# The last shifted copy of each VectorE quad made in place by an accumulating DMA from Pool

## The chip, the cores and the metric

The kernel runs on one core of one Trainium2 chip. The metric is the device time of one execution in microseconds; the median of three runs of the kernel before is 867.45 us (867.33 to 867.89). A change of the time is a change of that median.

## The reference

One transformer block with adaptive layer norm, 2048 tokens of 512 features, 32 heads of 16, a feed-forward layer of 1792, all in bf16:

```python
mod = (silu(c) @ w_mod).reshape(1, 6, 1, 512)        # sa, ca, ga, sb, cb, gb
h = layernorm(x) * (1 + ca) + sa
q, k, v = split(h @ wqkv)                            # 32 heads, 16 each
o = softmax(q @ k.T * 16 ** -0.5) @ v
x = x + ga * (o @ wo)
h = layernorm(x) * (1 + cb) + sb
x = x + gb * ((gelu(h @ w_gate) * (h @ w_up)) @ w_down)
```

The heavy part is the softmax: 32 x 2048 x 2048 exponentials (134 million), on 128 lanes.

## The kernel before

**Units, rounds, banks.** The query tokens are cut into six sets (SETS: three of 512, one of 256, two of 128). A *unit* is a set (or the two last ones together) and a group of four heads (`qd`, 0 to 7), so the four heads' keys share the 128 rows of TensorE. A *round* of a unit is one stretch of key tokens: its four scores (one for each head) fill four PSUM banks of 128 x 512. There are 2048 such banks in all, and `stream` emits them in chunks of up to three (CH = 3) into the two halves of the six-bank tile ps_sc. While ACT takes the exponential of one half into the ring E, TensorE writes the scores of the other.

**PV products.** After the exp, `pv_mms` multiplies the four banks of a round with the values (`vaug`, each head's 16 columns and a column of ones for the denominator) and accumulates the unit in ps_pv. When all rounds of a unit are done, `unit_end` copies ps_pv to osb, sends the denominators through two DRAM scratch tensors (SP's queue: scr_den, den, scr_rec, rb), and VectorE multiplies (onorm).

**Quads.** Part of the exponentials is made without ACT. For a round of keys at or beyond key tile T0 = 12, the four banks can be taken by VectorE: one `tensor_scalar` per bank (L338 is the helper that records it; L313 records matmuls, L326 activations) turns the score into the bits of a bf16 number, which is a piecewise linear approximation of the exponential. Such a round is a *quad*. Its bits lie in one of the NK = 3 buffers `kq` (128 x 2048 uint16: two in the tensor dreg, one in mreg). To smooth the approximation, the same bits are used five times: as they are, and with the four constants SHIFT = (26, 51, 77, 102) added to the bits. Each shifted copy is a `tensor_scalar` add over 128 x 2048 uint16 from `kq` into one of the NS = 4 buffers `sq` (in mreg), and is multiplied with the values scaled to match (`vs`). So a quad has five PV products instead of one; it costs VectorE four evictions of 128 x 512 from PSUM and four copies of 128 x 2048, and takes four banks off ACT. In a chunk that carries a bank of a quad, ACT's exp covers two banks (128 x 1024) in place of three (128 x 1536).

**The order is planned while the kernel is built.** The program is recorded by a planner that keeps a modelled clock for each engine (`free`), with a price for every instruction and DMA (`model`, L246), and emits each engine's instructions in a fixed order with semaphore waits. `stream` (L1117) is the loop: it takes the earliest thing that TensorE can do (scores of the next chunk, a PV product, side work, or a filler matmul that keeps TensorE busy), asking `probe` when the operands would be ready. VectorE's and SP's small steps wait in a list of tasks; `background` (L1032) lets SP and VectorE take those whose operands the model holds ready, by `urgency`. A quad is started or continued in a chunk only if the model has VectorE free soon enough:

```python
if len(mem) == CH and "modB" in self.have and self.free["dve"] < t + 700:
```

`shift_task` (L1391) enters the four shifted copies as VectorE tasks when the fourth bank has been evicted. A `kq` buffer comes free when all five products of the quad are done.

**Side work.** Projections of q, k, v, the output projection, the second layer norm and the feed-forward layer of earlier sets are generators (`plan`) whose matmuls go into the bank ps_mi between the chunks. What is left of the last sets' feed-forward layer runs in `tail` (L1455), after the last scores.

Of the kernel before, what the change touches and what calls it, by code (L numbers as in the profile page):

```python
# [6 lines left out]
ALU = mybir.AluOpType  # L7
# [4 lines left out]
U16 = mybir.dt.uint16  # L12

P = 128
# [20 lines left out]
CH = 3  # L35
# [2 lines left out]
assert NSL % CH == 0  # L38
LEAD = 5
T0 = 12  # L40
NK = 3
CREDIT = 1024
NS = 4
AHEAD = 24
FLOW = 3
URGENT = 9
# [11 lines left out]
SHIFT = (26, 51, 77, 102)  # L58
# [20 lines left out]
class _Recorder:  # L79
# [166 lines left out]
    def model(self, op, t, cost):  # L246
        eng = op.eng
        if op.stream not in COMPUTE:
            size, run = cost
            self.free[eng] = t + 450  # L250
            self.dma_free = max(t + 900, self.dma_free) + size / (320 if run >= 1024 else 245 if run >= 512 else 200)
            op.t1 = self.dma_free + (1000 if run > 64 else 1500)
        elif eng == "pe":
            cols, rows, tp = cost
            mode = 0 if tp is None else (1 if rows == 32 else 2)
            t = max(t, self.pe_issue)
            if mode != self.pe_mode:
                t = max(t, self.pe_end + 105)
            q = range(16)
            if mode == 1:  # L260
                q = range(tp[0] // 8, tp[0] // 8 + 4)
            elif mode == 2:
                q = range(tp[1] // 32, 16, 4)
            t = max(t, max(self.tile_free[i] for i in q))
            end = t + max(cols, 64) / 2.4
            for i in q:
                self.tile_free[i] = end
            self.pe_mode, self.pe_issue, self.pe_end = mode, t + (4 if mode else 27), max(self.pe_end, end)
            self.free[eng] = t
            self.log.append((t, cols if mode == 0 else cols / 4))  # L270
            op.t1 = end + 158
        else:
            self.free[eng] = t + cost
            op.t1 = t + cost + (107 if eng == "act" else 92)
# [93 lines left out]
    def bn_aggr(self, out, in_):  # L368
        return self.rec("dve", lambda e: e.bn_aggr(out, in_), [in_], [out], cost=90)

    def dma(self, eng, out, in_, sem, noncontig=False):
        def fn(e):
            if noncontig:
                with self.nc.allow_non_contiguous_dma(reason="small strided transfer"):
                    return e.dma_start(out, in_)
            return e.dma_start(out, in_)  # L376
        n = mybir.dt.size(out.dtype)
        for _, k in out.ap:
            n *= int(k)
        run = min(int(a.ap[-1][1]) * mybir.dt.size(a.dtype) for a in (out, in_))  # L380
        return self.rec(eng, fn, [in_], [out], dma=sem, cost=(n, run))

    def emit(self, final):
        for s in self.count:
# [34 lines left out]
class _Kernel(_Recorder):  # L419
# [12 lines left out]
    def alloc(self):  # L432
# [14 lines left out]
        mreg = sb("mreg", [P, 2 * NDC * F], BF16)  # L447
        self.wst = [[mreg[:, 1024 * (2 * x + b):1024 * (2 * x + b) + 1024].rearrange("p (a n) -> p a n", a=NDC)
                     for b in range(2)] for x in range(2)]
        self.sq = [mreg[:, 4096 + 2048 * i:6144 + 2048 * i] for i in range(NS)]  # L450
        self.wmod = mreg[:, 0:NDC * 3072].rearrange("p (a n) -> p a n", a=NDC)
        dreg = sb("dreg", [P, NFC * D], BF16)
        self.tb1 = dreg[:, 0:8 * D].rearrange("p (b t n) -> p b t n", b=2, t=4)
# [6 lines left out]
        self.wu += [dreg[:, 1024 * i:1024 * i + 1024].rearrange("p (a n) -> p a n", a=NDC) for i in range(4, 7)]  # L460
        self.wd = [self.xs[:, 2 * i:2 * i + 2, :] for i in range(6)]
        self.wd.append(hreg[:, NFC * 256 + 1024:NFC * 256 + 2048].rearrange("p (f n) -> p f n", f=2))
        self.kq = [dreg[:, 0:2048], dreg[:, 2048:4096], mreg[:, 12288:14336]]
        self.vs = sb("vs", [P, len(SHIFT), NKT - T0, H * VW], BF16)
        self.wo = sb("wo", [P, 8, D], BF16)
        self.E = sb("E", [P, NSL, 512], BF16)
# [26 lines left out]
        self.mi = ps("ps_mi", [P, 512], FP32)  # L493
        self.scr1 = self.dram("scr_den", [4, 2048], FP32)
        self.scr2 = self.dram("scr_rec", [4, 2048], FP32)


    def prologue(self):
        sp, act, pe, dve, pool = "sp", "act", "pe", "dve", "pool"
# [20 lines left out]
        self.memset(dve, self.pv[:, :], 0.0)  # L520
        self.memset(dve, self.scp[:, SC - 1, :], 0.0)
        self.warm_up(7)
        self.memset(pool, self.ident[:, :], 0.0)
        self.affine_select(self.ident[:, :], [[-1, P]], ALU.not_equal, 1.0, 0, 1)
        self.memset(pool, self.rm4, 1.0)
# [4 lines left out]
        self.memset(pool, self.vaug[:, :, :].rearrange("p t (h c) -> p t h c", c=VW)[:, :, :, DH:VW], 1.0)  # L530
        self.memset(pool, self.rb[:, :], 0.0)

        for dc in range(NDC):
            self.mm(self.scp[:, 0, dc:dc + 1], self.crow[0:1, P * dc:P * dc + P], self.ones[0:1, 0:1])
        self.act(self.tcol[:, :], self.scp[:, 0, 0:NDC], ACT.Tanh, scale=0.5)
# [494 lines left out]
        return n  # L1030

    def background(self, t):  # L1032
        while self.step("sp", max(self.free["sp"], t) + 40):
            pass
        while self.free["dve"] <= t + 150 and self.step("dve", max(self.free["dve"], t) + 40):
            pass

    def force(self):
        if not self.step("sp", None) and not self.step("dve", None):
            assert self.step("act", None)  # L1040

    def plan(self, ends, nsplit):
# [74 lines left out]
    def stream(self):  # L1117
# [26 lines left out]
        for u in units[2:]:  # L1144
            n, kpb = NKT * u[3] // 512, 512 // u[3]
# [12 lines left out]
        group = {u: max(0, i - 1) for i, u in enumerate(units)}  # L1158
        cg = 0
        left = {u: 0 for u in units}  # L1160
        for u, r, g0 in rounds:
# [3 lines left out]
        quads = []  # L1165
        wait = []
        self.quad_free = list(range(NK))
        self.sq_free = list(range(NS))
        cand = [k for k, (u, r, g0) in enumerate(rounds)
                if u not in units[:2] and r * (512 // u[3]) >= T0]  # L1170
        quad = None

        def take(n):
            r, i = [], pos
# [56 lines left out]
        def pv_do(x):  # L1231
            nonlocal rp, cg
            _, kind, k, rnd, i, src, q = x
            u = rnd[0]
            pv(rnd, i, src)
            begun.add(u)
            left[u] -= 1
            if kind == 0:
                assert k == next(open_rounds())
                rp = k + 1  # L1240
                self.plain[u] -= 1
            else:
                q["ready"].remove((i, src))
                q["n"] -= 1
                if i:
                    self.sq_free.append(q["slots"].pop(i))
                if q["n"] == 0:
                    wait.remove(q)
                    self.quad_free.append(q["k"])
            if left[u] == 0:  # L1250
                self.unit_end(u, acc_of(u))
                if all(left[v] == 0 for v in units if group[v] == cg):
                    cg += 1

        early, late = self.weight_parts()
        while cg <= group[units[-1]]:
# [16 lines left out]
            if tq is not None and tq <= t + 30:  # L1273
# [6 lines left out]
                    self.mm(self.scp[:, s0, :], *filler)  # L1280
                    continue
                g = None
                if len(mem) == CH and "modB" in self.have and self.free["dve"] < t + 700:
                    while quad is None and cand and rounds[cand[0]][2] < pos + AHEAD:
                        cand.pop(0)
                    overdue = {x[1][1] for x in self.tasks if x[1] is not None and x[1][0] == "shift" and self.plain[x[1][1]] <= LATE}
                    if quad is not None:
                        if not overdue - {quad["rnd"][0]}:
                            g = quad["rnd"][2] + quad["j"]
                    elif (not overdue and cand and self.quad_free and (pos < ends[2] or self.credit < CREDIT) and rounds[cand[0]][2] < pos + 96 and self.backlog() < BACK  # L1290
                          and ("vs", rounds[cand[0]][0][1] // 2) in self.have
                          and all(k in self.have for k in self.keys(seq[rounds[cand[0]][2]]))):
                        rnd = rounds[cand.pop(0)]
                        quad = {"rnd": rnd, "j": 0, "k": self.quad_free.pop(0), "ready": [], "n": NS + 1, "slots": {}}
                        left[rnd[0]] += NS
                        self.plain[rnd[0]] -= 1
                        g = rnd[2]
                        vec.update(range(g, g + 4))
                        mem, after = take(CH)
# [14 lines left out]
                if g is not None:  # L1314
                    j = quad["j"]
                    kq = self.kq[quad["k"]]
                    self.ts("dve", kq[:, 512 * j:512 * j + 512].bitcast(U16), self.scp[:, s0 + n, :], 128 / OCT, SHIFT_C,
                            ALU.mult, ALU.add)
                    quad["j"] = j + 1
                    if j == 3:  # L1320
                        quad["ready"].append((0, [kq[:, 512 * x:512 * x + 512] for x in range(4)]))
                        wait.append(quad)
                        for i in range(NS):
                            self.shift_task(quad, i)
                        quad = None
                if self.work and pos >= self.work[0][1]:
# [11 lines left out]
            if w is not None and pos >= w[1]:  # L1338
                ts = self.probe(w[4][1])
                n = w[4][0]  # L1340
# [50 lines left out]
    def shift_task(self, q, i):  # L1391

        def f():
            s = self.sq_free[0]
            self.ts("dve", self.sq[s].bitcast(U16), self.kq[q["k"]].bitcast(U16), float(SHIFT[i]), None, ALU.add)
            if self.probing is None:
                self.sq_free.pop(0)
                q["slots"][i + 1] = s
                q["ready"].append((i + 1, [self.sq[s][:, 512 * x:512 * x + 512] for x in range(4)]))
        self.task([f], ("shift", q["rnd"][0]), lambda: bool(self.sq_free))  # L1400

    def osb_span(self, u):

# [197 lines left out]
```

## Time and profile before

| | before |
|---|---|
| median of 3 runs | 867.45 us (867.33 to 867.89) |
| profiled execution, span | 868.7 us |
| ACT busy | 834.9 us, 96% |
| PE busy | 801.4 us, 92% |
| DVE (VectorE) busy | 694.5 us, 80% |
| POOL busy | 4.5 us |
| mean granted TensorE clock | 0.996 |
| ACT exps from ps_sc, three banks / two banks | 380 / 312 |
| DVE evictions of a quad's bank / shifted copies | 284 / 284 |

The profiled execution has no time of its own beside its span; the span is 1.25 us above the median of the runs. PE is the matmul side of TensorE, PEld its weight loads, ACT ScalarE, DVE VectorE, POOL GpSimd, SP the engine that issues nearly all DMAs. An instruction's duration includes a part in which it overlaps its predecessor on the same engine, so durations of one engine can add up to more than its busy time. In a list of groups each row has the line, the engine, the operation, the tiles (out <- in), the count, then busy us and mean ns of one, and the idle time before it with what ended it. In a list of waits each row has who waited for whom, us in total, how often, and the longest. 71 quads follow from the 284 evictions.

### The profile page before, as it was taken

The numbers are of one execution on the slowest core, as the hardware profiler recorded it, in microseconds if no ns is written. First come the engines' busy times: TensorE is split into PE (matmuls) and PEld (weight loads), VectorE is DVE, ScalarE is ACT, GpSimd is POOL, SyncE is SP. The second block draws the span as 40 slices with busy tenths as digits, with TensorE's granted clock in tenths as the row PEclk, the third lists the DMA queues.
The fourth block names the chain that finished last, engine by engine and source line by source line (L and its number), as shares of the span: only waits on it lengthen the run. The fifth ranks groups of instructions, "written<-read, shape, count | busy, mean of one in ns | idle before, by whom it ended". The sixth has DMA issues, their size and how long they took to land.

```text
span 868.7 us, 27825 instructions
## 1 busy us (share of the span) xinstructions
PE 801.4 (92%) x12558; PEld 283.4 (33%) x12563; DVE 694.5 (80%) x1315; ACT 834.9 (96%) x746; POOL 4.5 (1%) x12
## 2 busy tenths in 40 slices
PE   7889999999998999999999999999998899988977
PEld 3333332322222222222222222222343233345555
DVE  6855788888889899989899999988987674586574
ACT  4999999999999999999999999999999999999992
POOL 1000000000000000000000000000000000000000
PEclk9999999999999999999999999999999999999999
DMA  8101000000001212110001212120234231500000
GB/s 272 45 17 24 6 9 9 10 9 8 3 15 42 78 33 57 45 45 21 15 15 50 70 33 57 34 57 8 59 91 118 68 85 37 151 13 8 21 6 13
DMA packets 63665, 38.08 MB, mean 44 GB/s; under 512 B 17374, under 2 KB 61403, under 8 KB 63547
## 3 DMA queue, kind: packets, MB, share of 16 engines
q1 hardware_dynamic: 63544, 36.31, 14.6%
q8 instruction: 98, 1.61, 0.8%
q14 instruction: 21, 0.16, 0.1%
q10 hardware_dynamic: 2, 0.00, 0.0%
HBM read 33.68 MB, written 2.61 MB: 42 GB/s over the span
## 4 chain that ended last, share of the span: by engine, by line
ACT 78%; PE 14%; DVE 4%; DMA 2%; SPq 1%; issue 1%; DVEq 0%
ACT E L326 76%; PE ps_sc L313 6%; PE ps_mi L313 5%; PE ps_pv L313 3%; ACT wreg L326 3%; DVE mreg L338 1%; DMA mreg<-in_w_mod_dram 1%; SPq L376 1%; DMA rb<-scr_rec 1%; DMA scr_rec<-rden 0%; DVE dreg L338 0%; DVE kme L338 0%; DVE wreg L330 0%; DVE kmo L338 0%; DVE st L366 0%
## 5 line engine op out<-in xcount | busy, mean ns | idle before, releaser
L326 ACT ACTIVATE E<-ps_sc 128x1536 bf16<-128x1536 f32 (+2 forms) x698 | 808.3, 1355 | 13.8 <-PE ps_sc L313 13.6
L313 PE MATMUL ps_sc<-qT,kmo 32*128 32x512 bf16 (+2 forms) x1408 | 179.5, 323 | 12.4 <-ACT E L326 11.1
L313 PE MATMUL ps_sc<-qT,kme 32*128 32x512 bf16 (+2 forms) x1344 | 177.6, 332 | 13.4 <-ACT E L326 10.5
L313 PE MATMUL ps_pv<-E,vaug 128*17 128x512 bf16 (+2 forms) x2360 | 173.5, 322 | 4.2 <-ACT E L326 2.3
L338 DVE TENSOR_SCALAR dreg<-ps_sc 128x512 uint16<-128x512 f32 x192 | 132.5, 690 | 35.3 <-PE ps_sc L313 33.0
L338 DVE TENSOR_SCALAR mreg<-dreg 128x2048 uint16<-128x2048 uint16 x192 | 125.7, 681 | 1.6 <-PE ps_pv L313 1.6
L313 PE MATMUL ps_mi<-wreg,mreg 128*32 128x512 bf16 (+2 forms) x1600 | 109.2, 361 | 9.7 <-DVE wreg L343 4.0
L313 PE MATMUL ps_pv<-mreg,vs 128*17 128x512 bf16 (+2 forms) x1312 | 99.4, 351 | 1.8 <-DVE mreg L338 1.2
L313 PEld LDWEIGHTS ps_sc<-qT,kme 32*128 32x128 bf16 x1344 | 46.3, 91 | 133.7 <-ACT E L326 103.5
L313 PEld LDWEIGHTS ps_sc<-qT,kmo 32*128 32x128 bf16 x1408 | 48.4, 91 | 126.6 <-ACT E L326 100.6
L313 PEld LDWEIGHTS ps_pv<-E,vaug 128*17 128x17 bf16 x2360 | 53.4, 89 | 94.1 <-issue 64.2
L338 DVE TENSOR_SCALAR mreg<-ps_sc 128x512 uint16<-128x512 f32 x92 | 63.4, 690 | 17.9 <-PE ps_sc L313 16.8
L338 DVE TENSOR_SCALAR mreg<-mreg 128x2048 uint16<-128x2048 uint16 x92 | 61.2, 684 | 0.2 <-PE ps_pv L313 0.2
L313 PEld LDWEIGHTS ps_mi<-wreg,mreg 128*32 128x32 bf16 x1600 | 33.4, 95 | 60.4 <-issue 20.4
L347 DVE CAST wreg<-ps_mi 128x512 bf16<-128x512 f32 x51 | 35.0, 687 | 17.9 <-PE ps_mi L313 17.8
L343 DVE SCALAR_TENSOR_TENSOR wreg<-wreg,ps_mi 128x512 bf16<-128x512 bf16 x51 | 34.8, 683 | 11.1 <-PE ps_mi L313 7.6
L313 PEld LDWEIGHTS ps_pv<-mreg,vs 128*17 128x17 bf16 x1312 | 29.9, 89 | 30.8 <-DVE mreg L338 14.2
L313 PE MATMUL ps_mi<-hreg,wreg 128*32 128x512 bf16 x480 | 38.5, 383 | 0.7 <-DVE vaug L347 0.3
L313 PE MATMUL ps_mi<-wo,onorm 128*32 128x512 bf16 x480 | 37.4, 383 | 0.2
L330 DVE TENSOR_TENSOR wreg<-wreg 128x1024 bf16<-128x1024 bf16 (+1 forms) x60 | 35.7, 603 | 0.7
L313 PE MATMUL ps_sc<-xs,ident 128*32 128x512 bf16 (+1 forms) x281 | 25.0, 385 | 9.2 <-ACT E L326 8.9
L330 DVE TENSOR_TENSOR onorm<-osb,rb 128x512 bf16<-128x512 f32 (+2 forms) x43 | 23.6, 549 | 11.9 <-DMA rb<-scr_rec 11.6
(144 smaller groups left out, 591.3 us busy)
## 6 DMA issues: line engine op xcount, KB each, us to landing
mreg<-in_B_w_up_dram SPq DMA_DIRECT2D x25, 256.0 KB, 3.3
mreg<-in_B_w_gate_dram SPq DMA_DIRECT2D x21, 256.0 KB, 2.9
rb<-scr_rec SPq DMA_DIRECT2D x96, 32.0 KB, 1.8
mreg<-in_B_w_down_dram SPq DMA_DIRECT2D x12, 256.0 KB, 2.7
dreg<-in_B_w_down_dram SPq DMA_DIRECT2D x9, 256.0 KB, 4.0
mreg<-in_w_mod_dram SPq DMA_DIRECT2D x1, 2048.0 KB, 12.3
out_dram<-xs SPq DMA_DIRECT2D x16, 128.0 KB, 1.7
xs<-in_A_x_dram SPq DMA_DIRECT2D x3, 512.0 KB, 6.4
```

Source lines behind the costliest of these rows:

```text
L313: return self.rec("pe", lambda e: e.matmul(out, lhsT, rhs, start=start, stop=stop, tile_position=tp), [lhsT, rhs], [out], cost=(n, int(rhs ...
L326: return self.rec("act", lambda e: e.activation(out, in_, func, scale=scale, **kw), rd, wr, cost=self.cost("act", out, [in_], "act"))
L330: return self.rec(eng, lambda e: e.tensor_tensor(out, a, b, op), [a, b], [out], cost=self.cost(eng, out, [a, b], "tt"))
L338: return self.rec(eng, lambda e: e.tensor_scalar(out, a, s1, s2, **kw), rd, [out], cost=self.cost(eng, out, [a], "ts") + (60 if len(rd) > ...
L343: return self.rec("dve", lambda e: e.scalar_tensor_tensor(out, a, s, b, op0=op0, op1=op1), rd, [out], cost=self.cost("dve", out, [a, b], " ...
L347: return self.rec(eng, lambda e: e.tensor_copy(out, in_), [in_], [out], cost=self.cost(eng, out, [in_], "ts"))
L376: return e.dma_start(out, in_)
```

## The change

The kernel after has a fourth `kq` buffer (in the place of the fourth `sq` buffer, so there are NQ = 3 of those). Only three of a quad's four shifted copies are made as before. The fourth, the largest shift, is made in place: once the quad's plain PV product has been put on TensorE's queue, `last_task` enters a task that adds 102 to the bits in `kq` itself. While the unit still has at least FAR = 5 plain rounds to do, the task is a DMA issued by Pool with `accum_op=add`, whose source is a row of 2048 uint16 in DRAM, broadcast to the 128 partitions; otherwise it is a VectorE add in place. A copy that is made after the in-place add takes the difference of the shifts (`q["at"]`). The row in DRAM is written once, in the prologue, from a small memset in E. The planner's model has a price for such a DMA: it holds Pool for 1.5 us, and its result is there 6.5 us after its issue (DMA_ADD). `background` and `force` serve Pool's tasks as they do SP's. A unit that is not yet in turn must leave one `sq` buffer free. And the condition for VectorE's part in a chunk counts from ACT's time instead of TensorE's.

```diff
-NK = 3
+NK = 4
 CREDIT = 1024
 NS = 4
+NQ = 3
+DMA_ADD = 6500
+FAR = 5
...
             size, run = cost
+            if eng == "pool":
+                self.free[eng] = t + 1500
+                op.t1 = t + DMA_ADD
+                return
...
-    def dma(self, eng, out, in_, sem, noncontig=False):
+    def dma(self, eng, out, in_, sem, noncontig=False, add=False):
         def fn(e):
+            if add:
+                return e.dma_start(out, in_, accum_op=ALU.add)
...
-        return self.rec(eng, fn, [in_], [out], dma=sem, cost=(n, run))
+        return self.rec(eng, fn, [in_, out] if add else [in_], [out], dma=sem, cost=(n, run))
...
-        self.sq = [mreg[:, 4096 + 2048 * i:6144 + 2048 * i] for i in range(NS)]
+        self.sq = [mreg[:, 4096 + 2048 * i:6144 + 2048 * i] for i in range(NQ)]
...
-        self.kq = [dreg[:, 0:2048], dreg[:, 2048:4096], mreg[:, 12288:14336]]
+        self.kq = [dreg[:, 0:2048], dreg[:, 2048:4096], mreg[:, 12288:14336], mreg[:, 10240:12288]]
...
+        self.scrc = self.dram("scr_shift", [1, 2048], U16)
...
+        step = self.E[0:16, 0, 0:P].bitcast(U16)
+        self.memset(dve, step, SHIFT[NS - 1])
...
+        self.dma(pool, self.scrc.rearrange("o (p n) -> (o p) n", p=16), step, "cs")
...
-        while self.step("sp", max(self.free["sp"], t) + 40):
-            pass
+        for x in ("sp", "pool"):
+            while self.step(x, max(self.free[x], t) + 40):
+                pass
...
+        self.begun = lambda u: group[u] <= cg
...
-                if i:
+                if i == 0:
+                    self.last_task(q, self.plain[u] >= FAR)
+                if i in q["slots"]:
                     self.sq_free.append(q["slots"].pop(i))
...
-                if len(mem) == CH and "modB" in self.have and self.free["dve"] < t + 700:
+                if len(mem) == CH and "modB" in self.have and self.free["dve"] < max(t + 400, self.free["act"]) + 900:
...
-                        for i in range(NS):
+                        for i in range(NS - 1):
                             self.shift_task(quad, i)
...
-            self.ts("dve", self.sq[s].bitcast(U16), self.kq[q["k"]].bitcast(U16), float(SHIFT[i]), None, ALU.add)
+            self.ts("dve", self.sq[s].bitcast(U16), self.kq[q["k"]].bitcast(U16), float(SHIFT[i] - q["at"]), None, ALU.add)
...
-        self.task([f], ("shift", q["rnd"][0]), lambda: bool(self.sq_free))
+        self.task([f], ("shift", q["rnd"][0]), lambda: len(self.sq_free) > (not self.begun(q["rnd"][0])))
+
+    def last_task(self, q, far):
+
+        kq = self.kq[q["k"]]
+
+        def f():
+            if far:
+                self.dma("pool", kq.bitcast(U16), self.scrc.broadcast_to([P, 2048]), "ad%d" % q["k"], add=True)
+            else:
+                self.ts("dve", kq.bitcast(U16), kq.bitcast(U16), float(SHIFT[NS - 1]), None, ALU.add)
+            if self.probing is None:
+                q["at"] = SHIFT[NS - 1]
+                q["ready"].append((NS, [kq[:, 512 * x:512 * x + 512] for x in range(4)]))
+        self.task([("pool" if far else "dve", f)], ("add" if far else "shift", q["rnd"][0]))
```

More of the change, by code (lines that the diff above doesn't have):

```diff
@@ L1038, in force @@
     def force(self):
-        if not self.step("sp", None) and not self.step("dve", None):
+        if not self.step("sp", None) and not self.step("pool", None) and not self.step("dve", None):
             assert self.step("act", None)
@@ L1167, in stream @@
         self.quad_free = list(range(NK))
-        self.sq_free = list(range(NS))
+        self.sq_free = list(range(NQ))
         cand = [k for k, (u, r, g0) in enumerate(rounds)
@@ L1293, in stream @@
                         rnd = rounds[cand.pop(0)]
-                        quad = {"rnd": rnd, "j": 0, "k": self.quad_free.pop(0), "ready": [], "n": NS + 1, "slots": {}}
+                        quad = {"rnd": rnd, "j": 0, "k": self.quad_free.pop(0), "ready": [], "n": NS + 1, "slots": {}, "at": 0}
                         left[rnd[0]] += NS
```

## The prediction

> **What bounds the kernel now.** I read the page first: busy shares, then the chain that ended last.
>
> ```profile
> span 868.7 us, 27825 instructions
> PE 801.4 (92%) x12558; PEld 283.4 (33%) x12563; DVE 694.5 (80%) x1315; ACT 834.9 (96%) x746; POOL 4.5 (1%) x12
> ACT 78%; PE 14%; DVE 4%; DMA 2%; SPq 1%; issue 1%; DVEq 0%
> ```
>
> ACT is busy 96% of the span and carries 78% of the chain; Pool does nothing after the start. The second view, the groups by shape, gives the prices; the third, the waits, says who waits in the steady part.
>
> ```profile
> L326 ACT ACTIVATE E<-ps_sc 128x1536 bf16<-128x1536 f32 x380 | 543.4, 1557 | 1.5 <-PE ps_sc L313 1.4
> L326 ACT ACTIVATE E<-ps_sc 128x1024 bf16<-128x1024 f32 x312 | 316.8, 1125 | 3.4 <-PE ps_sc L313 3.4
> L338 DVE TENSOR_SCALAR dreg<-ps_sc 128x512 uint16<-128x512 f32 x192 | 132.5, 690 | 35.3 <-PE ps_sc L313 33.0
> L338 DVE TENSOR_SCALAR mreg<-dreg 128x2048 uint16<-128x2048 uint16 x192 | 125.7, 681 | 1.6 <-PE ps_pv L313 1.6
> ```
>
> ```profile
> DVE dreg L338 <- PE ps_sc L313: 33.0, 102, 1.2
> DVE mreg L338 <- PE ps_sc L313: 16.8, 49, 1.5
> ACT E L326 <- PE ps_sc L313: 13.6, 14, 2.1
> DVE onorm L330 <- DMA rb<-scr_rec: 11.6, 7, 4.2
> ```
>
> The exps wait before only a handful of their 692 runs, so ACT sets the pace. Each quad takes four banks off ACT: its four chunks have two banks instead of three. A table of windows (us from the start; PE, PEld, DVE, ACT, POOL busy, clock, DMA share, GB/s) shows where VectorE has room:
>
> ```profile
> 200.00:300.00 100.00, 93.37 (x1123) 26.15 (x1122) 88.60 (x160) 99.95 (x92) 0.00 (x0) 1.00 0.11 29
> 500.00:600.00 100.00, 94.36 (x1155) 25.75 (x1156) 90.89 (x151) 98.85 (x90) 0.00 (x0) 1.00 0.15 41
> 700.00:800.00 100.00, 92.76 (x1946) 40.70 (x1950) 63.98 (x136) 100.00 (x85) 0.00 (x0) 1.00 0.21 58
> ```
>
> Up to 600 us VectorE is about 90% busy, ACT full, PE at 93 to 94%. So three engines are near their limit together, and what is taken from one is soon asked of the next. The chunk pace is about 1.1 us (92 ACT instructions in 100 us).
>
> **The change, part by part.** Counts of the changed kernel come from the order of its built instructions.
>
> *More quads.* 71 quads become 79: 32 chunks go from three banks to two (1536-column exps 380 to 348, 1024-column ones 312 to 344). Each saves ACT 1557 - 1125 = 432 ns, in all 13.8 us. All of it lies on the chain.
>
> *VectorE.* 32 more evictions at 690 ns are +22.1 us; shifted copies fall from 284 to 250 (13 of them in place), 34 x 682 ns = -23.2 us. A wash: -1.1 us, not counted.
>
> *PE.* The additional quads' shifted products come to 24 more groups of four 512-column matmuls and 32 of 128 columns. At 0.21 us for a group that follows another (eight matmuls take 0.60 us in the timeline, four 0.39), the former are 5 us; the latter, at a quarter, 2 us. The 128x512 filler matmuls into ps_mi and ps_sc fall by 112, 28 groups or 6 us. A wash again, but fillers run only where PE is empty, so PE has that much less room to catch up. They also keep the clock up; with PE above 90% busy otherwise I price that at nothing.
>
> *Tail.* After the last score matmul the old order has 64 of the 128-column matmuls ps_mi<-wreg,mreg left; the new order has 128, and 64 of ps_mi<-wreg,qT more. So two more up-projection groups are still due when the exps end: the faster exp stream outruns the side work.
>
> ```profile
> 842.69 1.11 PE ps_mi L313 x64
> 845.00:868.70 23.70, 18.31 (x216) 13.16 (x219) 11.87 (x28) 5.16 (x11) 0.00 (x0) 1.00 0.04 12
> ```
>
> In the chain 64 such matmuls took 1.11 us, so two groups are 2.2 us; their VectorE and tanh steps (a 0.69 cast, a 0.69 product, five tensor products at 0.42, two 0.29 scalars, a tanh of 0.78) add 4.8 if nothing hides them. The window shows an idle ACT there, and no cover but the last sets' own work. Between 2.2 and 7.0 I take the middle, 4.5 us.
>
> *VectorE's turn later in a chunk.* An eviction may now start 0.90 us after ACT is free for the chunk, and ends at 1.59. The scores of that half of ps_sc can follow only then: 0.39 us of PE later is 1.98. A two-bank chunk and the next two-bank chunk take ACT 2 x 0.90 us (the timeline has four 1024-column exps in 3.79 us with the last one's 1.12: (3.79 - 1.12) / 3 = 0.89), so ACT idles 0.2, with the semaphores perhaps 0.3; behind a three-bank chunk nothing. In the old trace 151 of 284 evictions waited for their scores (102 + 49 above), so most are not late. I let the 32 new ones be late, half of them before a two-bank chunk: 16 x 0.3 = 5 us, between 0 and 10 if all 32 pay.
>
> *66 accumulating DMAs.* Each adds one 4 KB row, read 128 times, onto 128 x 2048 uint16 (512 KB). No row shows such a DMA, nor any issued by Pool. The nearest:
>
> ```profile
> mreg<-in_B_w_up_dram SPq DMA_DIRECT2D x25, 256.0 KB, 3.3
> mreg<-in_w_mod_dram SPq DMA_DIRECT2D x1, 2048.0 KB, 12.3
> xs<-in_A_x_dram SPq DMA_DIRECT2D x3, 512.0 KB, 6.4
> dreg<-in_B_w_up_dram SPq DMA_DIRECT2D x3, 256.0 KB, 5.3
> ```
>
> Below, half the bytes land in 3.3 us; above, source, old value and result together are 1.5 MB, under the 2 MB of w_mod with 12.3 us. I take 6.4, the row with the same destination size, which shared its queues at the start. The planner lays the order out for DMA_ADD = 6.5 us: it puts the products that need the sum at the first moment when it believes them there. Between an add and the first PE matmul that waits for it stand 3 or 4 chunks for 4 adds, 5 for 15, 6 for 15, 7 for 17, and 8 to 12 for 15; at 1.1 us, five are 5.5 to 6.6 us with the broken ones at the ends. So an early landing gains nothing, and a late one stalls PE, which is in order: behind the waiting product stand the scores of the next chunks, and ACT runs dry once its one filled half of ps_sc is done (0.90 to 1.33 us). In 25 cases VectorE waits for a landing too, with evictions behind it. The same load lands at 3.3 and at 5.3 us above, a spread of 2. With a mean of 6.4 and half that spread either way, I let 34 adds (those with six chunks or fewer) lose 0.2 us on average after the reserve: 7 us. Ends: 0 if all land in time; 24 if those 34 run 1 us late and lose 0.7 each.
>
> On SP's side 39 chains of small DMAs (scr_den, den, scr_rec, rb) now meet the adds on the same engines. Seven waits of VectorE for rb cost 11.6 us before. If the seven become ten, each 0.5 us longer and the new ones as long as one old wait's third, that is some 3 us; 0 to 10.
>
> Weighed against the skill: Pool's row is 4.5 busy us, all near the start, so no row shows Pool beside VectorE's 2048-column copies. The Trainium skill, SBUF — State Buffer, section "SBUF: two separate sides", says that a DMA from GpSimd waits for its descriptors while VectorE runs a two-port operation. By that rule, landings would come up to a copy or two later, which is the third rival.
>
> *At nothing:* the first DMA that writes the addend (Pool ends its memsets at 5.14 us, the first exp reads and writes at 17.67; 12 us of cover); the fourth buffer (it only lets a quad stay longer); the uint16 memset.
>
> Sum: -13.8 + 4.5 + 5 + 7 + 3 = +5.7 us without the rule. The span of 868.7 is 1.25 us above the median 867.45, so the difference is applied to the median: 873.2, rounded to 873.
>
> **Rivals.** About 0.2% (1.7 us) can be told from no change.
>
> 1. *The adds land inside the plan, with no trouble on SP's queue.* -13.8 + 4.5 + 5 = -4.3: 863.1 us. For it: 256 KB loads at 3.3 us, a DMA share of 0.11 to 0.15 in the main stage. Against it: nothing in the order gives margin. Decided by landings under 6.5 us. The Trainium skill, DMA: Bandwidth & Descriptors, section "Anatomy of one DMA — SWDGE (gpsimd) path", fits 2.0 us plus bytes at 436 GB/s, an estimate of 3.2 us for a plain copy of this size; by it the plan would hold, but no run here shows the accumulating kind. Chance 0.30.
> 2. *Losses and gain cancel within 1.7 us.* 867.5 us. Chance 0.15.
> 3. *Landings at 8 us or more.* A descriptor writer held up by VectorE's copies, or a third pass over the bytes: 6.4 and two copies at 0.68 are 7.8. At 8, 1.5 past the plan, 51 adds with seven chunks or fewer lose 1.5 less half a chunk (0.6), 0.9 each, 46 us in place of the 7: 867.5 + 5.7 + 39 = 912 us. The Trainium skill's rule above would speak for it. Chance 0.15.
>
> **The numbers.** The forecast, slower by 2 to 23 us, has 0.40: own range 869.2 to 890. Faster 0.30, same 0.15, slower 0.55. The range runs from 862 to 893: it leaves out rival 3 and the best end of rival 1.
>
> **What would show it.** Exps 348 and 344; the PE waits for DMA into dreg and mreg a new row of several us, ACT's waits for ps_sc far above 13.6 us; the add's landing near 6.4 us. Wrong if ACT's waits stay below 20 us and no engine waits for the adds (rival 1), or if the landing row says 8 or more (rival 3). The tail is wrong if the time from the last exp of three banks or two to the end does not grow.

## The result and the profile after

The changed kernel takes 945.55 us (median of four runs, 943.22 to 950.23) beside 867.39 us of the kernel before: a ratio of 1.0905, interval 1.0875 to 1.0935. It is 78 us slower; the forecast was 873, range 862 to 893. The direction was right and the size was not.

The page of the changed kernel, its head:

```profile
span 943.5 us, 28158 instructions
PE 838.3 (89%) x12675; PEld 293.1 (31%) x12675; DVE 695.8 (74%) x1314; ACT 831.5 (88%) x746; POOL 65.9 (7%) x79
PE 41%; ACT 22%; DMA 19%; DVE 13%; SPq 3%; issue 2%; DVEq 0%
ACT E L333 21%; PE ps_sc L320 15%; PE ps_mi L320 14%; PE ps_pv L320 11%; DMA scr_rec<-rden 7%; DMA rb<-scr_rec 7%; DVE mreg L345 3%; DMA den<-scr_den 3%; SPq L385 3%; DMA mreg<-scr_shift 2%; DVE dreg L345 1%; DVE onorm L337 1%; DVE osb L354 1%; DVE wreg L350 1%; DVE wreg L337 1%
```

VectorE is as busy as it was (695.8 us, 694.5 before) and ACT a little less; both are idle for longer. PE is busy for 37 us more, but hardly by more work: e9 below has the same matmuls without the stalls and 807.0 us (801.4 before); the rest goes with a lower clock (last section). Pool's 65.9 us are nearly all the issues of the adds. The chain says where the time is: ACT's share is down from 78% to 22%, and DMA has 19%. But read which DMAs: the accumulating ones (scr_shift) have 2%. The rest is scr_rec, rb and den, the small transfers that carry the softmax denominators through DRAM. The change did not touch them.

The waits of the changed kernel (who waited for whom: us in total, times, longest):

```profile
ACT E L333 <- PE ps_sc L320: 82.5, 83, 5.0
DVE onorm L337 <- DMA rb<-scr_rec: 59.6, 22, 6.4
PEld ps_pv L320 <- DVE mreg L345: 42.9, 41, 6.0
PE ps_pv L320 <- DVE mreg L345: 29.2, 14, 5.5
DVE rden L357 <- DMA den<-scr_den: 7.6, 9, 1.4
PEld ps_pv L320 <- DMA mreg<-scr_shift: 6.0, 5, 2.2
PEld ps_pv L320 <- DMA dreg<-scr_shift: 4.7, 5, 1.1
PE ps_pv L320 <- DMA mreg<-scr_shift: 4.1, 3, 1.9
PE ps_pv L320 <- DMA dreg<-scr_shift: 3.1, 5, 0.8
```

Read from the bottom up, these rows separate two effects. TensorE waits for the adds themselves for about 11 us on its weight loads (PEld), and 7 us on its matmuls. VectorE waits 59.6 us for rb, 11.6 before. TensorE's wait for shifted copies (mreg) and ACT's wait for scores (82.5 us, 13.6 before) follow: VectorE is in order, so while it stands at the onorm product, the shifted copies behind it are not made.

The small transfer whose result rb reads, in the list of issues (how many, KB each, median us to landing), before and then after:

```profile
scr_rec<-rden SPq DMA_DIRECT2D x24, 8.0 KB, 1.4
```

```profile
scr_rec<-rden SPq DMA_DIRECT2D x24, 8.0 KB, 3.6
```

One stall shows it engine by engine. The timelines of SP, POOL, DVE, PE and ACT (start, us, what, idle before):

```profile
199.49 0.34 SPq L385 DMA_DIRECT2D scr_rec<-rden  x1
205.33 1.71 SPq L385 DMA_DIRECT2D rb<-scr_rec  x4
```

```profile
197.49 1.73 POOL L381 DMA_DIRECT2D mreg<-scr_shift  x2 [17.06 <-PE ps_pv L320]
205.78 0.85 POOL L381 DMA_DIRECT2D dreg<-scr_shift  x1 [6.56 <-PE ps_pv L320]
```

```profile
211.91 0.69 DVE L337 TENSOR_TENSOR onorm<-osb,rb 128x512 bf16<-128x512 f32 x1 [6.45 <-DMA rb<-scr_rec]
212.52 1.89 DVE L345 TENSOR_SCALAR mreg<-mreg 128x2048 uint16<-128x2048 uint16 x3
```

```profile
213.27 1.21 PE L320 MATMUL ps_pv<-mreg,vs 128*17 128x512 bf16 x8 [5.16 <-DVE mreg L345]
```

```profile
215.06 1.45 ACT L333 ACTIVATE E<-ps_sc 128x1536 bf16<-128x1536 f32 x1 [5.04 <-PE ps_sc L320]
```

Two adds are issued at 197.49 and about 198.35. SP issues scr_rec, 8 KB, at 199.49, and rb, which reads what scr_rec wrote, can go only at 205.33: scr_rec took 5.8 us, where such a transfer had taken 1.4 in the median before. By the trace's landings the second add was there at 205.14 and scr_rec at 205.31. The next add goes out at 205.78 among the four rb transfers and lands at 211.42; the last rb lands at 211.79. VectorE has then stood 6.45 us, PE 5.16, ACT 5.04.

What the DMA engines did meanwhile is in the table of windows, whose last three columns are the granted clock, the DMA share and GB/s (packets on one engine overlap a little, so the share can pass 1):

```profile
200.00:202.00 2.00, 1.59 (x26) 0.43 (x23) 1.84 (x4) 2.00 (x2) 0.00 (x0) 1.00 1.10 215
208.00:210.00 2.00, 0.11 (x4) 0.00 (x0) 0.00 (x0) 2.00 (x2) 0.00 (x0) 1.00 1.01 188
212.00:214.00 2.00, 0.73 (x8) 0.20 (x8) 2.00 (x4) 0.00 (x0) 0.00 (x0) 0.61 0.00 0
```

While the adds move, the 16 engines are full on average.

The accumulating DMAs did what the planner counted on in two cases of three (44 of 66 landed within 6.5 us, from the trace's landings). Size and median time to landing:

```profile
dreg<-scr_shift POOLq DMA_DIRECT2D x34, 512.0 KB, 5.5
mreg<-scr_shift POOLq DMA_DIRECT2D x32, 512.0 KB, 5.9
```

The view of that tile gives 4.8, 5.7 and 8.9 us as shortest, median and longest landing.

### The profile page after: what moved, and what is told of

Same layout as the page of the kernel before. It is cut to its first block, busy times and chain, and to the rows that moved or that the text cites. A ratio compares the mean times of both kernels' runs of the same rounds, so it can differ in the third digit from the quotient of the medians.

```text
span 943.5 us, 28158 instructions
## 1 busy us (share of the span) xinstructions
PE 838.3 (89%) x12675; PEld 293.1 (31%) x12675; DVE 695.8 (74%) x1314; ACT 831.5 (88%) x746; POOL 65.9 (7%) x79
## 3 DMA queue, kind: packets, MB, share of 16 engines
q0 software_dynamic: 9536, 34.61, 19.9%
q1 hardware_dynamic: 63544, 36.31, 13.8%
## 4 chain that ended last, share of the span: by engine, by line
PE 41%; ACT 22%; DMA 19%; DVE 13%; SPq 3%; issue 2%; DVEq 0%
ACT E L333 21%; PE ps_sc L320 15%; PE ps_mi L320 14%; PE ps_pv L320 11%; DMA scr_rec<-rden 7%; DMA rb<-scr_rec 7%; DVE mreg L345 3%; DMA den<-scr_den 3%; SPq L385 3%; DMA mreg<-scr_shift 2%; DVE dreg L345 1%; DVE onorm L337 1%; DVE osb L354 1%; DVE wreg L350 1%; DVE wreg L337 1%
## 5 line engine op out<-in xcount | busy, mean ns | idle before, releaser
L333 ACT ACTIVATE E<-ps_sc 128x1536 bf16<-128x1536 f32 (+2 forms) x698 | 802.3, 1275 | 83.9 <-PE ps_sc L320 82.5
L320 PE MATMUL ps_sc<-qT,kmo 32*128 32x512 bf16 (+2 forms) x1408 | 186.3, 331 | 9.4 <-ACT E L333 6.4
L320 PE MATMUL ps_sc<-qT,kme 32*128 32x512 bf16 (+2 forms) x1344 | 185.5, 341 | 8.3 <-ACT E L333 6.4
L345 DVE TENSOR_SCALAR dreg<-ps_sc 128x512 uint16<-128x512 f32 x164 | 111.9, 689 | 33.3 <-PE ps_sc L320 32.3
L320 PE MATMUL ps_mi<-wreg,mreg 128*32 128x512 bf16 (+2 forms) x1600 | 115.8, 375 | 16.0 <-DVE wreg L350 8.0
L345 DVE TENSOR_SCALAR mreg<-ps_sc 128x512 uint16<-128x512 f32 x152 | 103.0, 688 | 21.5 <-PE ps_sc L320 20.1
L345 DVE TENSOR_SCALAR mreg<-dreg 128x2048 uint16<-128x2048 uint16 x123 | 81.7, 686 | 6.4 <-PE ps_pv L320 6.2
L345 DVE TENSOR_SCALAR mreg<-mreg 128x2048 uint16<-128x2048 uint16 x120 | 79.2, 684 | 5.1 <-PE ps_pv L320 3.6
L337 DVE TENSOR_TENSOR onorm<-osb,rb 128x512 bf16<-128x512 f32 (+2 forms) x43 | 23.6, 550 | 59.6 <-DMA rb<-scr_rec 59.6
L381 POOL DMA_DIRECT2D dreg<-scr_shift x34 | 31.5, 936 | 429.7 <-PE ps_pv L320 311.5
L381 POOL DMA_DIRECT2D mreg<-scr_shift x32 | 30.5, 964 | 313.6 <-PE ps_pv L320 250.8
```

The costliest lines, as they stand in the source:

```text
L320: return self.rec("pe", lambda e: e.matmul(out, lhsT, rhs, start=start, stop=stop, tile_position=tp), [lhsT, rhs], [out], cost=(n, int(rhs ...
L333: return self.rec("act", lambda e: e.activation(out, in_, func, scale=scale, **kw), rd, wr, cost=self.cost("act", out, [in_], "act"))
L337: return self.rec(eng, lambda e: e.tensor_tensor(out, a, b, op), [a, b], [out], cost=self.cost(eng, out, [a, b], "tt"))
L345: return self.rec(eng, lambda e: e.tensor_scalar(out, a, s1, s2, **kw), rd, [out], cost=self.cost(eng, out, [a], "ts") + (60 if len(rd) > ...
L381: return e.dma_start(out, in_, accum_op=ALU.add)
```

## The experiments

Theory A: the adds fill the DMA engines, the small DMAs of the denominators land late beside them, VectorE stands in order at the product that needs them, and TensorE and ACT run dry behind it. Rival B: the later turn or the buffers are at fault. Rival C: the descriptors that Pool writes (the prediction's third rival, without late landings). Rival D: the adds' own late landings. All ratios are against the kernel before.

**e1: no adds from Pool.**

```diff
-FAR = 5
+FAR = 100
```

> The changed kernel with FAR = 100: every in-place add is made by VectorE (a fifth... fourth 2048-column copy again), no DMA from Pool but the one in the prologue; the fourth buffer and the later turn stay; the planner makes a new order with 75 quads. Theory A (the 66 DMAs cost the time, through whatever they collide with): 863 to 872 us, VectorE's waits for rb back near 12 us. Rival B (the later turn or the three shifted-copy buffers cost it): 900 us or more, and waits of ACT for ps_sc stay near 80 us.

867.46 us, ratio 0.9992 (0.9966 to 1.0019). Without the DMAs the loss is gone, with the fourth buffer, the later turn and 75 quads in place, and VectorE's wait for rb is 10.1 us. B falls. The planner's order is another one here, so this run says which part costs, not how.

**e2: the same order, a sixteenth of the bytes.**

```diff
-                return e.dma_start(out, in_, accum_op=ALU.add)
+                return e.dma_start(out[:, 0:P], in_[:, 0:P], accum_op=ALU.add)
```

> The order of the changed kernel to the instruction, but each accumulating DMA moves only the first 128 of its 2048 columns (32 KB in place of 512 KB, the same 128 rows to describe); the other columns stay without the shift. Theory A (bytes of the adds on the shared DMA engines make the small DMAs of the denominators late, and VectorE stands behind them): 860 to 872 us, landings of the small DMAs back at 1.4 to 1.8 us, VectorE's waits for rb 10 to 20 us. Rival C (the descriptors that Pool writes for each DMA, or what writing them does to VectorE, cost the time): the rows are as many, so over 920 us remains. Rival D (the adds themselves land late): the same 860 to 872 us, but then the small DMAs' landings in the run tell nothing; e3 tells A from D.

870.51 us, ratio 1.0018 (0.9993 to 1.0043). The waits of e2:

```profile
ACT E L333 <- PE ps_sc L320: 22.8, 28, 2.5
DVE onorm L337 <- DMA rb<-scr_rec: 12.0, 12, 2.6
```

The order of the instructions, what each waits for and the number of rows to describe are those of the changed kernel (Pool is busy for 66.1 us, 65.9 there), and nearly all of the loss is gone. C falls: it is the moved data, not the descriptors that Pool writes. A and D both expected this; scr_rec at 2.0 us (8 KB) landed a little later than the 1.4 to 1.8 that A had named.

**e3: the same adds, SP's DMAs priced later in the plan.**

```diff
             op.t1 = self.dma_free + (1000 if run > 64 else 1500)
+            if self.count.get("d_cs"):
+                op.t1 += 2000 if size <= 65536 else 1500
```

> The changed kernel, but once the prologue is over the planner prices every DMA of SP later: 2.0 us more for those of 64 KB or less, 1.5 us more for the larger ones, and so puts their consumers later; the adds' price (6.5 us) and FAR stay, 65 adds and 74 quads come out. Theory A (VectorE stands behind small DMAs that land later than planned): the wait rows of VectorE for rb fall from 59.6 to under 25 us and the time to 880 to 905 us, though three adds fewer than... one add fewer is made and five quads fewer are taken off ACT. Rival D (late adds cost it): 930 us or more, since they are priced as before.

887.76 us, ratio 1.0209 (1.0165 to 1.0252). The adds are as many but one, of the full size, and no better priced; the onorm products stand later in VectorE's queue. Three quarters of the loss go, and VectorE's wait for rb is down to 15.9 us. That is A's mark, not D's. But the order is another one, with 74 quads for 79, so the next three runs keep the order.

**e5: VectorE waits for no rb.** The normalisation is left out of the product; the order, the adds and the small DMAs stay.

```diff
-            self.tt("dve", self.onorm[:, qd, c:c + W], osb, rb, ALU.mult)
+            self.loose = "d_dd"      # planned as if it read rb; no wait for rb
+            self.rec("dve", lambda e: e.tensor_tensor(out, osb, osb, ALU.mult), [osb, rb], [out], ...)
+            self.loose = None
```

> The order of the changed kernel to the instruction; only VectorE's onorm product reads osb twice in place of osb and rb (the normalisation is left out there), so it waits for no landing of rb. The 66 adds with all their bytes and the chains of small DMAs run as they did. Theory A (VectorE's in-order wait for rb carries most of the loss): 870 to 895 us, since the waits of TensorE for the adds (18 us) and for the reciprocals (8 us) are left. Rival D (the adds' own landings, past 6.5 us for the slower ones, carry it): 920 us or more.

886.81 us, ratio 1.0198 (1.014 to 1.0257), inside A's range.

**e6: TensorE waits for no add.** The quads' last product reads the tensor wo in place of the bits.

```diff
+                if i == NS:
+                    self.loose = "d_ad"      # planned as if it read kq; reads wo, no wait for the add
+                    self.rec("pe", lambda e, ...: e.matmul(o, l, other, ...), [l, r2, other], [o], ...)
+                    self.loose = None
+                    continue
```

> The order of the changed kernel to the instruction; only the quads' last product reads the tensor wo in place of the bits with the add, so TensorE waits for no add (that part of the softmax is replaced by other data). Theory A: VectorE's waits for rb stay near 60 us and the time is 915 to 945 us. Rival D: 880 us or less.

935.80 us, ratio 1.0757 (1.0706 to 1.0808). So in one and the same order, taking VectorE's wait for rb away brings 7 points back, taking TensorE's wait for the adds away 1.5. A carries the loss and D is a small second part.

**e9: neither waits.** Both edits together.

> The order of the changed kernel to the instruction, with the edits of e5 and e6 together: VectorE's onorm product reads no rb (no normalisation there) and the quads' last product reads wo, so neither waits for a DMA that the adds made late or for the adds. If these two waits are the whole loss: 866 to 876 us. If late weight loads, the reciprocals' loads or PE's lower clock carry a part of their own: 880 us or more.

873.24 us, ratio 1.0034 (1.0005 to 1.0063). The waits of e9:

```profile
ACT E L336 <- PE ps_sc L323: 26.6, 34, 2.7
DVE rden L360 <- DMA den<-scr_den: 11.7, 12, 2.1
```

The small DMAs land as late as in the changed kernel (scr_rec 3.5 us for those of 8 KB), and SP's queue waits for scr_rec as long (95.3 us in total, 92.8 there, 41.2 before), but the loss is gone. What stays is VectorE's wait for den, another of the small DMAs, at 11.7 us (3.0 before); it cost little.

The sum closes. From e9, giving back the wait for the adds costs 1.0198 - 1.0034 = 1.6 points (14 us), giving back the wait for rb 1.0757 - 1.0034 = 7.2 points (63 us); together 1.0034 + 0.0164 + 0.0723 = 1.092, measured 1.0905. By the intervals the sum is good to about 0.8 points. For all else, late weight loads included, e9 leaves 0.3 points (3 us).

**e7: a plain copy in place of the add,** same order, same bytes written (the last product then gets constants).

```diff
-                return e.dma_start(out, in_, accum_op=ALU.add)
+                return e.dma_start(out, in_)
```

> The order of the changed kernel to the instruction; the DMAs from Pool copy the row of constants over the bits and do not add (the last product then gets constants). If the bytes written are what crowds the small DMAs: landings of 5 to 6 us as before and 930 to 950 us. If the second read (the old value) is a good part of it: landings under 4.5 us and 870 to 910 us.

879.96 us, ratio 1.0127 (1.0097 to 1.0158), inside the second range; landings 3.6, 4.2 and 6.9 us. VectorE's wait for rb is 17.6 us. The queue of Pool's DMAs, first in the changed kernel and then in e7 (packets, MB, share of 16 engines' span):

```profile
q0 software_dynamic: 9536, 34.61, 19.9%
```

```profile
q0 software_dynamic: 9536, 34.61, 11.3%
```

The packets and bytes are the same; a packet takes 0.199 x 943.5 us x 16 / 9536 = 315 ns of an engine when it adds and 0.113 x 874.2 x 16 / 9536 = 166 ns when it copies. Adding nearly doubles the engines' time, and the loss grows sevenfold, from 1.3 to 9 points (1.6 of them by late adds, which e7 doesn't have: one of its copies landed after 6.5 us, and no engine waited for it). That fits a plan with a little slack: beside copies scr_rec of 8 KB lands in 2.2 us and VectorE waits for rb 14 times, beside adds in 3.6 and 22 times (1.4 and 7 before).

**e8: a source row for each partition,** in place of one row read 128 times.

```diff
-                self.dma("pool", kq.bitcast(U16), self.scrc.broadcast_to([P, 2048]), "ad%d" % q["k"], add=True)
+                self.dma("pool", kq.bitcast(U16), self.scrw, "ad%d" % q["k"], add=True)
```

> The order of the changed kernel on every engine but Pool, which in the prologue fills a DRAM tensor of 128 rows with the constant; each add reads 128 rows of its own in place of one row 128 times. If the shared 4 KB row in DRAM slows the adds: landings under 5 us and 880 to 920 us. If it doesn't matter: landings at 5.5 to 6 us and 935 to 955 us.

956.12 us, ratio 1.0994 (1.0913 to 1.1074), a microsecond past the second range; landings 5.3, 5.8 and 9.0 us. The shared row is not what slows the adds.

**e12: everything priced as it lands.** e3's prices, DMA_ADD = 8500 and FAR = 7.

> The changed kernel with every DMA priced as the traces of this case show it beside adds: SP's small DMAs 2.0 us later, its larger ones 1.5 us later, the adds at 8.5 us, and FAR = 7; 46 adds and 74 quads come out. If mispriced landings are the whole loss, and an order that is laid out for them costs what its fewer free slots cost: 872 to 884 us, VectorE's waits for rb under 15 us. If adds cost something that no order can hide: above 890 us.

877.75 us, ratio 1.0089 (1.0061 to 1.0117), and VectorE's wait for rb is 8.5 us. A plan that knows these landings hides most of what the adds cost, but then 46 of them and 74 quads are left, and it is still behind the kernel before.

**e4, e10, e11: the later turn alone,** without DMA from Pool, on the kernel before: limits of 900, 700 and 500 ns behind the later of ACT's free time and 400, 600 and 400 ns from now. All three have 74 quads. e11's edit:

```diff
-                if len(mem) == CH and "modB" in self.have and self.free["dve"] < t + 700:
+                if len(mem) == CH and "modB" in self.have and self.free["dve"] < max(t + 400, self.free["act"]) + 500:
```

> The kernel before with the later turn alone: the condition for VectorE's part in a chunk as in the changed kernel, three bit buffers, four shifted-copy buffers, no DMA from Pool; 74 quads in place of 71. If late evictions cost 5 us as the prediction had it, while 12 chunks of ACT lose 0.43 us each (5 us): 867 us, within 2. If the later turn is free: 862 to 864 us. If it is the harmful part of the change: over 880 us.

> The kernel before with the later turn alone, but a limit of 700 ns behind the later of ACT's free time and 600 ns from now (e4: 900 and 400); 74 quads. No DMA from Pool. If the gain of e4 (0.25%) comes from three more quads, the same again: 864 to 867 us, ratio 0.996 to 0.999. If late evictions cost something in e4, the smaller limit gives more: ratio under 0.996.

> The kernel before with the later turn alone, limit 500 ns behind the later of ACT's free time and 400 ns from now; 74 quads. By the three more quads alone: ratio 0.996 to 0.999. If late evictions cost something in e4: ratio under 0.996.

| | median us | ratio | interval |
|---|---|---|---|
| e4, 900 / 400 | 866.26 | 0.9975 | 0.9958 to 0.9992 |
| e10, 700 / 600 | 863.33 | 0.9924 | 0.9895 to 0.9952 |
| e11, 500 / 400 | 862.11 | 0.9908 | 0.9876 to 0.9940 |

e11 beats both kernels. Its page and groups:

```profile
span 859.7 us, 27909 instructions
L326 ACT ACTIVATE E<-ps_sc 128x1536 bf16<-128x1536 f32 x368 | 519.4, 1549 | 1.3 <-PE ps_sc L313 1.2
L326 ACT ACTIVATE E<-ps_sc 128x1024 bf16<-128x1024 f32 x324 | 320.6, 1127 | 2.6 <-PE ps_sc L313 2.4
```

Twelve chunks have lost a bank, 12 x 0.42 = 5 us of ACT; the ratio is worth 8 us, and where the other 3 come from was not separated. e10 and e11 both came out under 0.996, as expected if late evictions cost something. That the tighter limits do better with the same number of quads fits the prediction's price on late evictions, but the orders differ in other ways too, so it isn't shown.

## Why the prediction was wrong

**Right.** Exps 348 and 344; VectorE with as much work as before (695.8 us, 694.5 before), and PE with nearly as much (807.0 us in e9, 801.4 before; fewer fillers for more products); the first DMA of the addend hidden. The landing was taken as 6.4 us and is 5.7 in the median. The tail: from the end of the last exp of three banks to the end it was 844.10 to 868.7, 24.6 us; in the changed kernel it is 911.54 to 943.5, 32.0, and in e2, which has the same order without the crowd, 840.56 to 872.1, 31.5; in e7 and e9, with that order too, it is 30.1 and 29.6. So 5 to 7 us where 4.5 was taken, with 7.0 as its upper bound.

**ACT's gain,** priced at 13.8 us less 5 for late evictions, came out smaller. In e2 the last exp of three banks ends only 3.5 us earlier than before: ACT is busy for 10.9 us less (824.0 us), but waits for scores for 9.2 us more (22.8 us, 13.6 before).

**The step that failed** is the sentence on SP's small DMAs: "If the seven become ten, each 0.5 us longer [...] that is some 3 us; 0 to 10." Measured: 63 us. It named the right place and the right waiter and had the size wrong by twenty, in two ways. (By its own figures the sum is 5 us, not 3: seven times 0.5, and three times a third of 1.7.) It let each wait grow by 0.5 us; beside an add scr_rec's median is 3.8 us (24 of 39 transfers, from the trace's landings) where it had been 1.4, and rb's 2.9 in place of 1.8. And it took the number of waits from the old profile: seven in 39 chains. But the planner puts the onorm products close to the moment at which it believes rb landed. In the old trace rb had landed only 1.5 us (median of 43 products) before its product began, and 34 of the 43 had less than the 2.4 us by which scr_rec alone is late beside an add. A delay on a chain of four transfers, one behind the other, adds up at its end. 22 waits came out, 2.7 us each. The prediction said exactly this of the adds ("an early landing gains nothing, and a late one stalls PE, which is in order") and did not apply it to the DMAs that the planner places in the same way.

**Late adds.** 7 us were taken, with 0 to 24; e5 against e9 gives 14.

**The rivals.** Rival 1 had "no trouble on SP's queue" in its name, but named its point of decision as landings of the adds under 6.5 us. The median is under it, and the time still went the other way, because the point was set on the wrong DMAs. Rival 3 gave 912 us for landings at 8 us or more; the time went beyond that, but only 5 of the 66 adds took 8 us or more (8.9 is the longest), so it is not this case. The rule that stood behind it is from the Trainium skill, SBUF — State Buffer, section "SBUF: two separate sides": descriptors from GpSimd wait for VectorE's two-port operations. The trace of e7 fits it: the 19 of Pool's 66 DMAs whose issue met a VectorE copy of 2048 columns held Pool for 767 ns in the median (up to 1390), the others for 527 (up to 575). But that delay has no cost to be seen in the time: e2 has as many rows to describe beside as many copies, at 1.0018. The fit for a copy from the Trainium skill, DMA: Bandwidth & Descriptors, section "Anatomy of one DMA — SWDGE (gpsimd) path", would make 3.2 us of 512 KB (an estimate); e7's plain copies took 4.2 in the median from issue to landing, and 3.6 at the least.

**The range.** It had no case in which the crowd on the DMA engines was a cost of its own above 10 us. The old profile's DMA share of 0.11 to 0.15 was taken as room; the share is an average, and an add takes all engines at once for some microseconds (1.10 and 1.01 in the windows of the stall).

## What to carry to other kernels

When a bulk DMA is added beside chains of small dependent DMAs, price every transfer that shares the engines, not the new one alone, and then look for the in-order engine that stands at the end of the chain: what is queued behind that instruction pays, not the transfer. In a kernel whose order is fixed by planned times there is little slack to eat, so measure how long before its consumer each transfer lands instead of reading how rarely the consumers wait now. Test such a claim in the same order, by taking away one consumer's wait with other data, and check that the parts add up.

## What the runs showed of the hardware

A scr_rec transfer (8 KB or less, SP's queue) issued while 512 KB accumulating DMAs of Pool's queue were in flight never landed before the last of these, though the two have queues of their own. In the stall above it came 0.2 us after (205.31 and 205.14 us); of the 22 transfers issued like this, 16 landed within 0.25 us after the last such add and the other six 0.8 to 1.7 us after it.

The Trainium skill, DMA: Bandwidth & Descriptors, section "Queues, rings and completion order", has each engine take turns between queues packet by packet. The trace agrees. The data of an 8 KB scr_rec are 128 packets of 64 bytes. In the old trace they mostly passed within 0.2 us. In the stall they took from 202.26 to 204.81 us: 16 of them, as many as there are engines, in every 0.32 us, which is the time of one 4 KB packet of the add (328 ns). So a transfer cut into many small packets pays a whole packet of the other queue for each turn. It also began late, 2.8 us after its issue in place of 0.8; why is not shown.

An accumulating packet took an engine 315 ns on average, a copying one 166.

The stalls also went with a lower clock: the granted TensorE clock was 0.951 in the changed kernel and 0.996 before, and 512-column score matmuls took 398 to 401 ns in place of 384 to 386. In the stall shown it was 1.00 from 208 to 210 us and 0.61 from 212 to 214, after PE had stood for 5 us. In e9, the same order without the stalls, it was 0.992.
